# The same steps in another order: banded attention with block summaries, and a GELU MLP behind it

## The chip, the cores and the metric

The kernel runs on one core of a Trainium2 chip. The core has five engines that run side by side and meet only at semaphores: TensorE (PE) multiplies matrices, VectorE (DVE), ScalarE (ACT) and GpSimd (POOL) work on elements, and SyncE (SP) issues most of the transfers. The metric is the device time of one execution in microseconds (us). Runs of one kernel lie close together: the three of the kernel before lie between 559.98 and 560.04 us.

## What is computed

The reference, cut to what matters: an attention in which every query sees the keys less than 16 positions away and, beside them, one summary for each block of 32 keys (the maximum of the keys, the mean of the values), and an MLP with a GELU on its result.

```python
B, H, S, D = 4, 8, 768, 64;  block, window = 32, 16
k_sum = k.reshape(B, H, nb, block, D).max(axis=3)
v_sum = v.reshape(B, H, nb, block, D).mean(axis=3)
scores_l = where(abs(i - j) < window, q @ k.T / sqrt(D), -1e9)
scores_s = q @ k_sum.T / sqrt(D) + log(block)
a = softmax(concat(scores_l, scores_s));  out = a @ concat(v, v_sum)
x = out.transpose(0, 2, 1, 3).reshape(3072, 512)
h = x @ w_in                                  # w_in 512 x 2048
y = gelu(h) @ w_out                           # w_out 2048 x 512
```

## The kernel before

**Tiles.** The 3072 tokens are worked in batches (b, 0 to 3) and chunks of 256 tokens. The attention is cut into 24 units, each of four heads and four tiles of 64 queries; two units give one chunk of the MLP. PE multiplies 16-bit numbers: every 32-bit operand is split into a high and a low part (`_hi` on ACT or POOL, `_lo` on DVE), and a product of two operands is three matmuls. Chunks 0 to 3 of the MLP (argument c) go straight through `phase1`, `gelu` and `phase2`. The tokens behind them are multiplied by a scheme with sums and differences of blocks (Strassen's, `sp` for the first product and `so` for the second), which needs fewer matmuls and more work in sums: `xsum`, `snap`, `h_comb`, `h_gelu`, `h_sum`, `t_sum` and their `_hi` and `_lo` parts; `o_snap` (L1397), `o_sum` (L1404) and `o_out` (L1411) then collect the result from PSUM, and `o_put` (L1415) sends a piece of 128 by 256 numbers out.

**A unit's steps.** `scores` (PE, L861) multiplies queries and keys into the PSUM tile `pss`. `evac` (ACT, L877) or `add_mask` (DVE) fetch it, `maximum` (POOL, an all-reduce over partitions, L890), `shift` (DVE, L895) and `exponent` (ACT, L898) follow, then `s_p_hi`, `p_lo`, and on PE `values` and `sums`. `norm_take`, `norm_cross`, `norm_rec`, `norm_spread` and `norm_mult` divide by the sums, `x_hi` (ACT, L997) and `x_lo` (DVE, L1000) split the result for the MLP. A name with `f_` in front, `f_mask` and `m_shift` are the forms of the first three units; `s_k_hi` (ACT, L758) splits a unit's keys after `load_k` has brought them. `fill` steps are matmuls of ones, whose results nobody reads.

**The weights.** At the start DVE builds the split weights: `wi_bits` (three DVE steps, L477, L482, L486, for each of eight pieces that `fetch_w_in` brings), `wi_lo` (L515), `wo_bits`, `wo_lo` (L575), with `wi_hi` (L512) and `wo_hi` (L572) on ACT.

**What sets the order.** Nothing is scheduled by a planner on the way. `ORDER` (L79) is a string of 1,932 step names with arguments, and a loop at the end of the kernel calls them one after another. A step's instructions join the stream of their engine in this order, and each engine runs its stream in order; a DMA is issued by SP (or by ACT where the name has `a_` in front) in the order of its queue. Where two steps touch one tile the later in the list waits for the earlier. The table `SLOTS` says for each tag of small tiles (`f4k`, `g32`, `psh`, ...) which buffer the next tile of that tag takes, so that it depends on the order too. PSUM tiles are waited for as a whole: `o_snap b n j` reads the half j of the tile `pso_y`, `so b n q j` writes the half j, and a matmul that starts in one half waits for a reader of the other half that stands ahead of it.

In `so b n q j`, n is which of seven products (for one tile of results each), q the quarter of the inner dimension and j the half of 128 rows. With one and the same b and n, j the four quarters add up in the same PSUM tile. Six matmuls make one such step.

## Time and profile before

| | |
|---|---|
| time, median of three | 560.01 us (559.98 to 560.04) |
| the profiled execution | 560.75 us, of which the span is 558.9 us |
| granted TensorE clock, mean | 1.000 (2.4 GHz) |
| PE busy | 549.5 us (98%) |
| DVE busy | 484.0 us (87%) |
| ACT busy | 389.7 us (70%) |
| POOL busy | 110.8 us (20%) |
| bytes moved | 84.26 MB |

The profile cuts the span into stretches and says how long each engine was busy in each; it follows the chain of work that ended last back from the last instruction; and it lists the instructions of an engine in order of time, with the idle time ahead of each and what ended it. PE's busy time counts every matmul from its start to a modelled end, and matmuls overlap, so that PE can read as busy through a short gap; gaps are read from the starts.

### The profile page before, as it was taken

The page shows a single profiled execution, that of the slowest core. Times are in us where ns is not written, and L with a number is a line of the kernel's source. Part 1 is how long each engine was busy: PE and PEld are TensorE (multiplying, and loading weights), DVE is VectorE, ACT ScalarE, POOL GpSimd, SP SyncE. Part 2 cuts the span into 40 slices and gives each one's busy share as a digit, 9 for nine tenths or more (in the row PEclk, how much of TensorE's full clock was granted, in tenths as well). Part 3 has the DMA queues.
Part 4 walks back from the last instruction along what each step waited for, and adds up shares of the span by engine and source line. Part 5 has one row for each costly group of instructions (what it writes and reads, how often), then busy time and mean ns, then how long its engine had stood idle before and what let it go on. Part 6 is the DMA issues. An engine that isn't in the chain of part 4 may idle for free.

```text
span 558.9 us, 14486 instructions
## 1 busy us (share of the span) xinstructions
PE 549.5 (98%) x6155; PEld 414.8 (74%) x6155; DVE 484.0 (87%) x680; ACT 389.7 (70%) x677; POOL 110.8 (20%) x66
## 2 busy tenths in 40 slices
...
GB/s 328 396 285 380 166 173 178 280 116 221 157 146 171 153 143 187 133 65 182 127 167 149 154 115 89 90 145 200 256 207 150 60 94 1 1 1 29 48 1 86
DMA packets 42640, 84.26 MB, mean 151 GB/s; under 512 B 4176, under 2 KB 16720, under 8 KB 42064
## 3 DMA queue, kind: packets, MB, share of 16 engines
...
## 4 chain that ended last, share of the span: by engine, by line
PE 81%; DVE 13%; DMA 3%; issue 1%; ACT 1%; SPq 0%; DVEq 0%
PE psy L1091 15%; PE pso_y L1375 8%; PE psz L1091 8%; PE pso L1139 7%; PE pso L1140 7%; PE pso L1141 6%; PE psx L1091 4%; PE psd_y L1375 4%; PE pss_x L1375 4%; PE psv L943 3%; PE psh L1020 3%; PE psh L1021 2%; PE psh L1022 2%; PE pss L861 2%; PE psv_z L1375 2%; DMA w_out_h<-in_vt_dram 2%
## 5 line engine op out<-in xcount | busy, mean ns | idle before, releaser
L890 POOL PARTITION_ALL_REDUCE m<-s x23 | 82.0, 3567 | 187.4 <-DVE w_out_l L575 40.1
L1091 PEld LDWEIGHTS <-wt 128*128 128x128 f16 x768 | 74.3, 98 | 10.2 <-issue 0.2
L1139 PE MATMUL pso<-w_out_h,gg 128*128 128x512 f16 x192 | 72.9, 379 | 0.0
L1141 PE MATMUL pso<-w_out_h,gg 128*128 128x512 f16 x192 | 72.8, 379 | 0.0
L1140 PE MATMUL pso<-w_out_l,gg 128*128 128x512 f16 x192 | 72.8, 379 | 0.0
L1021 PE MATMUL psh<-xos,ww 128*128 128x256 f16 x256 | 69.8, 273 | 0.8 <-DVE xos L1000 0.8
L1091 PE MATMUL psy<-xos,wt 128*128 128x256 f16 x576 | 70.5, 273 | 0.0
L1020 PE MATMUL psh<-xos,ww 128*128 128x256 f16 x256 | 69.8, 273 | 0.1
L1022 PE MATMUL psh<-xos,ww 128*128 128x256 f16 x256 | 69.8, 273 | 0.0
L1091 PEld LDWEIGHTS <-ww 128*128 128x128 f16 x576 | 55.8, 98 | 8.9 <-issue 0.4
L1375 PEld LDWEIGHTS <-gg 128*128 128x128 f16 x576 | 55.8, 98 | 7.7 <-issue 1.1
L1102 ACT ACTIVATE ww<-psy 128x512 f32<-128x512 f32 x48 | 28.3, 591 | 27.4 <-PE psy L1091 27.3
L1141 PEld LDWEIGHTS <-gg 128*128 128x128 f16 x192 | 18.7, 98 | 22.8 <-issue 0.4
L1139 PEld LDWEIGHTS <-gg 128*128 128x128 f16 x192 | 18.7, 98 | 19.8 <-issue 0.4
L1140 PEld LDWEIGHTS <-gg 128*128 128x128 f16 x192 | 18.8, 98 | 19.1
L1375 PEld LDWEIGHTS <-wt 128*128 128x128 f16 x288 | 28.1, 98 | 3.4 <-issue 0.2
L1218 DVE SCALAR_TENSOR_TENSOR gg<-h,gg 128x512 f16<-128x512 f32 x32 | 21.4, 686 | 10.1 <-ACT gg L1215 9.9
L1020 PEld LDWEIGHTS <-ww 128*128 128x128 f16 x256 | 25.0, 98 | 4.3 <-issue 0.4
L1022 PEld LDWEIGHTS <-ww 128*128 128x128 f16 x256 | 25.0, 98 | 4.1 <-issue 1.2
L1021 PEld LDWEIGHTS <-ww 128*128 128x128 f16 x256 | 25.0, 98 | 3.7
L1029 ACT ACTIVATE g<-psh 128x512 f32<-128x512 f32 x32 | 19.0, 593 | 11.4 <-DVE gg L1038 8.6
L895 DVE TENSOR_TENSOR s<-s,m 128x1024 f32<-128x1024 f32 x21 | 25.5, 1216 | 0.1
...
## 6 DMA issues: line engine op xcount, KB each, us to landing
...
```

The source lines that it names most:

```text
L890: nc.gpsimd.partition_all_reduce(out_ap=self.m32, in_ap=self.s32, channels=P, reduce_op=bass_isa.ReduceOp.max)
L895: nc.vector.tensor_tensor(out=self.s32, in0=self.s32, in1=self.m32, op=ALU.subtract)
L1020: nc.tensor.matmul(ph[:, e, :], wh, xh, start=(k == 0), stop=False)
L1021: nc.tensor.matmul(ph[:, e, :], wh, xl, start=False, stop=False)
L1022: nc.tensor.matmul(ph[:, e, :], wl, xh, start=False, stop=(k == NCC - 1))
L1091: nc.tensor.matmul(ps[:, e, :], ws, xx, start=(first and e == 0 and k == 0 and m == 0), stop=(k == 1 and m == 2), skip_group_check=True,)
L1102: nc.scalar.activation(snaps[b, q, n], split8(acc[b, q, "y"]), AF.Copy)
L1139: nc.tensor.matmul(p, gh, w_out_h[:, f, :], start=(f == 0), stop=False)
L1140: nc.tensor.matmul(p, gh, w_out_l[:, f, :], start=False, stop=False)
L1141: nc.tensor.matmul(p, gl, w_out_h[:, f, :], start=False, stop=(f == NFC - 1))
L1218: nc.vector.scalar_tensor_tensor(out=a_part(b, q, m, 1), in0=h_src(b, q, m), scalar=SC_G, in1=a_part(b, q, m, 0), op0=ALU.mult, op1=ALU.su ...
L1375: nc.tensor.matmul(ps, g, ww_, start=(first and e == 0 and k == 0), stop=(e == 1 and k == 2), skip_group_check=True,)
```

## The change

The change moves steps in `ORDER` and writes `SLOTS` anew for that order. The list has the same 1,932 steps as before, and every engine has the same instructions; 1,726 steps stand at another place, most of them by a few places. No function is touched. Ten more lines of text in the table move the line numbers of all code behind it by 10: L1375 of before is L1385 of after. Two pieces of the diff:

```diff
-norm_take 1, x_lo 0, wi_bits 3 0, f_values 1, wi_bits 3 1, load_k 4, f_mask 3, norm_cross 1, scores 3, evac 3,
...
+norm_take 1, x_lo 0, wi_bits 3 0, wi_bits 3 1, f_mask 3, norm_cross 1, scores 3, s_k_hi 4, evac 3, norm_rec 1,
```

On ACT, near the start (some 34 us in): `evac 3` is the row with L877 (L887 after), `s_k_hi 4` the row with L758 (L768), `x_hi 1` the one with L997 (L1007), `wi_hi` the one with L512 (L522). Before:

```order
L877 ACTIVATE s32_3_456<-pss_3_399 128x1024
L512 ACTIVATE ww_93<-wt_94 128x8x128
L758 ACTIVATE k_all_100<-k32_4_397 128x10x64
L997 ACTIVATE xos_96<-x32s_95 128x512
L815 ACTIVATE qh_4_477<-q32_4_368 128x512
L512 ACTIVATE ww_93<-wt_94 128x8x128
```

And now:

```order
L768 ACTIVATE k_all_100<-k32_4_363 128x10x64
L887 ACTIVATE s32_3_442<-pss_3_384 128x1024
L522 ACTIVATE ww_93<-wt_94 128x8x128
L1007 ACTIVATE xos_96<-x32s_95 128x512
L825 ACTIVATE qh_4_477<-q32_4_353 128x512
L522 ACTIVATE ww_93<-wt_94 128x8x128
```

`s_k_hi 4`, which splits the keys that `load_k 4` brings, stood behind `evac 3` and `wi_hi 5` and now stands ahead of both; `x_hi 1` follows `wi_hi 5` directly.

On PE, where `so 3 4 0 0` and `so 3 4 0 1` begin (some 399 us in): L1091 (L1101) is a matmul of `sp 4 1 1` before and of `sp 4 0 1` now, and L1375 (L1385) the matmuls of the two `so` steps, six each; what a row waits for stands in brackets. Before:

```order
L1091 LDWEIGHTS ww_93
L1091 MATMUL psy_4_1_6274<-xos_96,ww_93 128x256
L1375 LDWEIGHTS gg_99 [waits DMAHW7_49]
L1375 MATMUL pso_y_3_5492<-wt_94,gg_99 128x256 [waits Activation_49]
...
L1375 LDWEIGHTS gg_99
L1375 MATMUL pso_y_3_5492<-wt_94,gg_99 128x256
L1375 LDWEIGHTS gg_99
L1375 MATMUL pso_y_3_5492<-wt_94,gg_99 128x256 [waits Activation_49]
```

And now:

```order
L1101 LDWEIGHTS ww_93
L1101 MATMUL psy_4_0_6282<-xos_96,ww_93 128x256
L1385 LDWEIGHTS gg_99 [waits DMAHW5_49]
L1385 MATMUL pso_y_3_5475<-wt_94,gg_99 128x256 [waits Activation_49]
...
L1385 LDWEIGHTS gg_99
L1385 MATMUL pso_y_3_5475<-wt_94,gg_99 128x256
L1385 LDWEIGHTS gg_99
L1385 MATMUL pso_y_3_5475<-wt_94,gg_99 128x256
```

Before, each of the two `so` steps waited for ACT, the second for `o_snap 3 3 1`, which stood between them in the list; now both `o_snap 3 3 0` and `o_snap 3 3 1` stand ahead of the first, and only the first waits. In the list `so 3 7 3 0`, `sp 4 1 1`, `o_snap 3 3 0`, `so 3 4 0 0`, `o_snap 3 3 1`, `so 3 4 0 1` has become `so 3 7 3 0`, `sp 4 0 1`, `o_snap 3 3 0`, `o_snap 3 3 1`, `so 3 4 0 0`, `so 3 4 0 1`.

On PE again, some 6 us from its end: `psd_y` is written by `so 5 7 3 1`, `pss_x` by `so 5 3 2 1` (its last row) ahead of it and by `so 5 3 0 1` behind it. Now:

```order
L1385 LDWEIGHTS wt_94
L1385 MATMUL pss_x_5_7934<-w_out_h_97,wt_94 128x256
L1385 LDWEIGHTS wt_94
L1385 MATMUL psd_y_5_7885<-t3_3_6597,wt_94 128x256
...
L1385 LDWEIGHTS wt_94
L1385 MATMUL psd_y_5_7885<-t3_3_6597,wt_94 128x256
L1385 LDWEIGHTS wt_94
L1385 MATMUL pss_x_5_7934<-w_out_h_97,wt_94 128x256 [waits DVE_49]
```

`o_sum 5 0` (DVE) reads the tile `pss_x`. It now stands between `so 5 3 2 1` and `so 5 7 3 1`, so that it waits for the former and `so 5 3 0 1` waits for it. Before, it stood ahead of `so 5 3 3 1`, `so 5 3 2 1` and `so 5 3 0 1` alike, with six matmul steps between it and the first of these, and that first one's row is the one that waited for it:

```order
L1375 MATMUL psv_z_5_8193<-w_out_l_98,gg_99 128x256
L1375 LDWEIGHTS gg_99
L1375 MATMUL psv_z_5_8193<-w_out_h_97,gg_99 128x256
L1375 LDWEIGHTS wt_94
L1375 MATMUL pss_x_5_7975<-w_out_h_97,wt_94 128x256 [waits DVE_49]
```

And on SP, the last issues of the program, all of them `o_put` (L1415, L1425 after). The tile `g32_os_5_1` is the result of `o_sum 5 0`, `g32_os_5_2` that of `o_sum 5 1`, `g32_os_5_3` that of `o_sum 5 3`, and `g32_os_5_5` those of `o_out 5 0` and `o_out 5 1`. Before:

```order
L1415 DMA out_0_dram<-g32_os_5_1_8065 128x256
L1415 DMA out_0_dram<-g32_os_5_3_8230 128x256
L1415 DMA out_0_dram<-g32_os_5_1_8065 128x256
L1415 DMA out_0_dram<-os_4_2_7417 128x256
L1415 DMA out_0_dram<-g32_os_5_3_8230 128x256
L1415 DMA out_0_dram<-g32_os_5_2_8158 128x256 x2
L1415 DMA out_0_dram<-g32_os_5_5_8342 128x256 x2
```

And now:

```order
L1425 DMA out_0_dram<-g32_os_5_1_8025 128x256
L1425 DMA out_0_dram<-g32_os_5_3_8192 128x256
L1425 DMA out_0_dram<-g32_os_5_5_8327 128x256
L1425 DMA out_0_dram<-g32_os_5_1_8025 128x256
L1425 DMA out_0_dram<-os_4_2_7506 128x256
L1425 DMA out_0_dram<-g32_os_5_3_8192 128x256
L1425 DMA out_0_dram<-g32_os_5_2_8139 128x256 x2
L1425 DMA out_0_dram<-g32_os_5_5_8327 128x256
```

The piece of `o_out 5 0` (the first row with `g32_os_5_5` now, `o_put 5 2 0`) has moved from next to last to the head of a row of seven issues; the piece of `o_out 5 1` is last in both.

## Rows read from the trace of the kernel before

**Rows 1.** The page, part 1: busy time, share of the span and instructions of each engine

```profile
PE 549.5 (98%) x6155; PEld 414.8 (74%) x6155; DVE 484.0 (87%) x680; ACT 389.7 (70%) x677; POOL 110.8 (20%) x66
```

**Rows 2.** Stretches (from:to, length), busy time of each engine, clock, DMA share, GB/s

```profile
20.00:40.00 20.00, 18.45 (x244) 10.78 (x241) 19.45 (x23) 16.13 (x34) 13.13 (x4) 1.00 0.90 330
...
120.00:140.00 20.00, 20.00 (x248) 11.48 (x247) 19.85 (x26) 14.57 (x23) 3.23 (x1) 1.00 0.63 187
...
380.00:420.00 40.00, 39.53 (x531) 33.66 (x530) 35.34 (x50) 28.24 (x54) 8.86 (x4) 1.00 0.76 225
...
540.00:559.00 19.00, 15.56 (x143) 13.70 (x140) 2.67 (x4) 1.43 (x4) 0.00 (x0) 1.00 0.19 63
```

**Rows 3.** The chain that ended last, 98 to 112 us (start, length, what)

```profile
107.81 0.70 DVE xos L1000
...
108.55 0.27 PE psh L1021
```

**Rows 4.** PE's waits: line, waited for, us in total, times, longest

```profile
PE pso_y L1375 <- ACT g_os L1397: 0.5, 1, 0.5
```

**Rows 5.** Order of time, PE, 398 to 402 us (start, length, line, operation, tiles)

```profile
398.93 0.82 PE L1375 MATMUL pso_y<-wt,gg 128*128 128x256 f16 x6
400.22 1.47 PE L1375 MATMUL pso_y<-wt,gg 128*128 128x256 f16 x12 [0.47 <-ACT g_os L1397]
```

**Rows 6.** Order of time, ACT, 398 to 402 us

```profile
399.78 0.38 ACT L1397 ACTIVATE g_os<-pso_y 128x256 f32<-128x256 f32 x1 [1.58 <-PE pso_y L1375]
```

**Rows 7.** Order of time, PE, 189.5 to 193 us

```profile
191.13 0.38 PE L1140 MATMUL pso<-w_out_l,gg 128*128 128x512 f16 x1
191.34 0.38 PE L1141 MATMUL pso<-w_out_h,gg 128*128 128x512 f16 x1
191.66 0.20 PE L861 MATMUL pss<-qh,k_all 64*128 64x64 f16 x2
```

**Rows 8.** Order of time, DVE, 377 to 389 us

```profile
381.93 0.69 DVE L1218 SCALAR_TENSOR_TENSOR gg<-g,gg 128x512 f16<-128x512 f32 x1 [1.06 <-ACT gg L1215]
...
384.87 0.69 DVE L1218 SCALAR_TENSOR_TENSOR wt<-g,wt 128x512 f16<-128x512 f32 x1
385.48 1.22 DVE L918 SCALAR_TENSOR_TENSOR vl<-v,vh 128x1024 f16<-128x1024 f32 x1
```

**Rows 9.** Order of time, PE, 386.5 to 388.5 us

```profile
387.68 0.38 PE L1375 MATMUL psh_w<-w_out_h,wt 128*128 128x256 f16 x2
```

**Rows 10.** Order of time, PE, 548 to 559 us

```profile
551.35 0.27 PE L1375 MATMUL pss_x<-w_out_h,wt 128*128 128x256 f16 x1
...
552.77 2.78 PE L1375 MATMUL psd_y<-t,gg 128*128 128x256 f16 x24
```

**Rows 11.** Order of time, DVE, 544 to 559 us

```profile
551.66 0.69 DVE L1404 SCALAR_TENSOR_TENSOR g_os<-pss_x,g_os 128x512 f32<-128x512 f32 x1 [0.61 <-PE pss_x L1375]
```

**Rows 12.** Order of time, SP's issues, 551 us to the end

```profile
551.35 0.45 SPq L1415 DMA_DIRECT2D out_dram<-os  x1
551.84 4.50 SPq L1415 DMA_DIRECT2D out_dram<-g_os  x5
...
556.00 0.33 SPq L1415 DMA_DIRECT2D out_dram<-g_os  x1
```

**Rows 13.** Order of time, ACT, 33 to 41 us

```profile
33.63 1.02 ACT L877 ACTIVATE s<-pss 128x1024 f32<-128x1024 f32 x1 [0.45 <-PE pss L861]
...
36.12 0.74 ACT L758 ACTIVATE k_all<-k 128x640 f16<-128x640 f32 x1 [0.38 <-DMA k<-in_kd_dram]
```

**Rows 14.** Order of time, DVE, 19.5 to 39 us

```profile
20.14 2.58 DVE L482 SCALAR_TENSOR_TENSOR wt<-x32s,wt 128x1024 int32<-128x1024 int32 x1
...
27.68 0.69 DVE L477 TENSOR_SCALAR wt<-gg 128x1024 int32<-128x1024 int32 x1 [0.28 <-DMA gg<-in_w_in_dram]
28.41 1.23 DVE L482 SCALAR_TENSOR_TENSOR wt<-gg,wt 128x1024 int32<-128x1024 int32 x1
...
38.54 0.68 DVE L1000 TENSOR_TENSOR xos<-x32s,xos 128x512 f16<-128x512 f32 x1
```

**Rows 15.** Order of time, POOL, 19.5 to 24 us

```profile
19.75 3.22 POOL L890 PARTITION_ALL_REDUCE m<-s  x1 [4.63 <-ACT s L877]
```

More of the change, by code (lines that the diff above doesn't have):

```diff
@@ L90 @@
-norm_rec 1, fetch_w_in 1 1, norm_spread 1, load_v 4, wi_hi 5, wi_bits 3 2, fill 10, s_k_hi 4, f_sums 2, norm_mult 1,
-x_hi 1, s_q_hi 4, norm_take 2, k_lo 4, wi_hi 3, x_lo 1, maximum 3, load_k 5, wi_lo 5, fill 2, wi_bits 1 0, f_mask 4,
-norm_cross 2, f_values 2, load_v 3, phase1 0 4, fetch_k 1 3, gelu 0 4, q_lo 4, phase1 0 0, wi_bits 1 1, phase1 0 5,
-shift 3, wi_hi 2, load_vs 3, wi_bits 1 2, norm_rec 2, load_vs 4, scores 4, exponent 3, norm_spread 2, wi_lo 3, wi_hi
-1, g_hi 0 4, fetch_w_in 6 2, norm_mult 2, prep_k 1 3, f_sums 3, wi_lo 2, gelu 0 0, norm_take 3, load_q 5, x_hi 2,
@@ L95 @@
-norm_cross 3, f_values 3, wi_lo 1, wi_bits 6 0, gelu 0 5, norm_rec 3, x_lo 2, fetch_k 1 0, fetch_w_in 7 3, norm_spread
-3, prep_k 1 0, evac 4, g_hi 0 5, maximum 4, norm_mult 3, phase1 0 3, s_k_hi 5, phase1 0 1, x_hi 3, fetch_w_out 0 4,
-g_hi 0 0, wi_bits 6 1, phase1 0 2, s_q_hi 5, k_lo 5, gelu 0 3, fetch_w_out 1 5, x_lo 3, phase1 1 4, q_lo 5, shift 4,
-exponent 4, wi_bits 6 2, load_k 6, g_lo 0 4, f_mask 5, gelu 0 1, wo_bits 0 0, s_k_hi 6, f_sums 4, g_lo 0 0, scores 5,
-wo_bits 0 1, wi_bits 7 0, load_v 5, g_hi 0 3, g_lo 0 5, f_values 4, gelu 0 2, g_hi 0 1, phase1 1 1, wo_bits 0 2,
@@ new lines @@
+norm_take 2, wi_hi 3, k_lo 4, x_lo 1, maximum 3, load_k 5, load_v 4, fill 2, wi_lo 5, wi_bits 1 0, f_mask 4,
+norm_cross 2, f_values 2, load_v 3, phase1 0 4, gelu 0 4, fetch_w_in 6 2, q_lo 4, phase1 0 0, phase1 0 5, wi_bits 1 1,
+shift 3, wi_hi 2, load_vs 3, wi_bits 1 2, norm_rec 2, norm_spread 2, load_vs 4, exponent 3, f_sums 3, wi_lo 3, scores
+4, wi_hi 1, g_hi 0 4, norm_mult 2, prep_k 1 3, wi_lo 2, load_q 5, x_hi 2, gelu 0 0, norm_take 3, wi_bits 6 0, f_values
+3, fetch_k 2 1, wi_lo 1, norm_cross 3, phase1 0 3, fetch_k 1 0, fetch_w_in 7 3, x_lo 2, norm_rec 3, g_hi 0 0, g_lo 0
```

395 lines of the change are left out of this document (205 added, 190 removed).

## The prediction

> **What bounds the kernel now.** I read the page's busy times first: PE is busy for 549.5 of 558.9 us, DVE for 484.0 [rows 1]. That says that PE bounds the kernel as a whole, not that it does so everywhere. The stretches tell it apart: from 20 to 40 us PE is busy for 18.45 of 20 us and DVE for 19.45, so the start is paced by DVE, which builds the split weights; from 120 us on PE is busy all the time (20.00 of 20), with one dent, 39.53 of 40 us from 380 to 420 [rows 2]. The chain of work that ended last shows where the one regime passes into the other: DVE's `x_lo 5` runs from 107.81 us, and the matmul of `phase1 2 6` that needs it starts at 108.55 us; from there the chain is PE's [rows 3]. So there are three places where an order can gain or lose: DVE's work ahead of `x_lo 5` and what stretches it, gaps on PE behind 108.55 us, and what follows PE's last matmul. The clock was at its full level (1.00) in every stretch read here [rows 2], so no term comes from it.
>
> On PE a gap shows in the distance of two starts. The matmuls of `so 3 4 0 0`, six of them, start from 398.93 us, and at the 0.11 us at which such matmuls follow each other the next would start at 399.59; it starts at 400.22 [rows 5]. That is a gap of 0.63 us, the only wait for another engine that the list of waits shows with L1375 [rows 4]: `o_snap 3 3 1` runs from 399.78 for 0.38 us, released by PE itself [rows 6].
>
> **The change, step by step.** No instruction comes or goes, so PE's own work is the same, and only waits, gaps and the two ends count.
>
> 1. The start: 0. Ahead of `x_lo 5` DVE has the very same instructions in both orders, and so has PE ahead of `phase1 2 6`; they stand in another order among themselves. DVE is all but never idle there, so the sum of durations sets when `x_lo 5` ends, and the order can change it only through DVE's idle time (one wait of 0.28 us for a transfer of weights) and through operations that last longer beside POOL: one `wi_bits` operation took 2.58 us beside an all-reduce that runs from 19.75 to 22.97 us, where its like takes 1.23 [rows 14, 15]. Which operations meet an all-reduce changes with the order in both directions. I take 0, and one such meeting more or fewer, plus or minus 1.35 us, as the bounds.
>
> The Trainium skill (SBUF — State Buffer, Who interferes with whom) says that GpSimd and some DVE operations share a pair of ports under an exclusive lock, and that the loser is blocked for the whole of the other's instruction. By that one meeting could cost up to the 3.22 us of the all-reduce; the row shows 1.35 us, so the measured stretch is what I use, and by the page alone the bounds would be 3.2 us to either side.
>
> 2. `so 3 4`: -0.63. Both `o_snap`s now stand ahead of `so 3 4 0 0`, and `sp 4 0 1` (12 matmuls, 12 x 0.11 = 1.31 us) stands between `so 3 7 3 0`, which releases them, and `so 3 4 0 0`. The last matmul's own 0.27 us, two copies of 0.38 [rows 6] and about 0.1 of handing over make 1.13 us behind that matmul's start, and PE arrives 0.11 + 1.31 = 1.42 us behind it. The wait goes, with 0.3 us to spare; ahead of the copies ACT has `exponent 21` and `s_p_hi 21`, which by the work ahead of them are through about a microsecond earlier.
>
> 3. `so 5 3 0 1`: +0.29. `o_sum 5 0` now waits for `so 5 3 2 1`, and `so 5 3 0 1` for `o_sum 5 0`. An `o_sum` takes 0.69 us and starts 0.31 behind the start of the matmul it waits for (551.35 to 551.66) [rows 10, 11]; with 0.05 to hand over PE may go on 1.05 us behind that matmul. In between it has only `so 5 7 3 1`, 6 x 0.11 = 0.65, and the 0.11 of the matmul itself: 0.76. The difference, 0.29 us, stands on PE with nothing behind it to hide it.
>
> 4. Switches: +0.5. Where PE goes from 128 x 128 matmuls to an attention block, it loses time without waiting for anyone: the matmuls start 0.21 us apart (191.13, 191.34), and the first of `scores` comes 0.32 us behind the last of them (191.66) [rows 7], 0.1 us more. I counted the places in the two orders behind `phase1 2 6`: 37 before, 42 after. Five more are 0.5 us; the trace shows such a gap at nearly all places of before.
>
> 5. `h_lo 3 3 4`: +0.3. Before, it runs from 384.87 to 385.56 us, and the matmul that needs it at 387.68 [rows 8, 9]. Now three operations more stand between `h_lo 3 3 12` (381.93) and it, `v_lo 20` with 1.22 us and two of the size of an `h_lo`, 0.69 each, 2.6 us in all [rows 8], and its matmul is 0.65 us earlier (one step fewer is ahead of it). If `h_lo 3 3 12` starts where it did, the part is ready at 388.1 at most and the matmul waits up to 1.0 us. But DVE idled 1.06 us ahead of `h_lo 3 3 12`, for ACT, [rows 8]; one sum of 0.68 us moves into that idle time, and so the chain behind it can run that much earlier. Between 0 and 1.0 I take 0.3, since the earlier chain takes 0.7 off the 1.0.
>
> 6. The end: +0.3. PE's last matmul ends at 552.77 + 2.78 = 555.55 us, and the last issue of SP is at 556.00, 0.45 behind it [rows 10, 12]. SP's issues follow each other at 0.49 us (551.35, 551.84) when released [rows 12]. Now `o_put 5 2 0`, which needs `o_out 5 0`, heads a row of seven issues. Four matmul steps stand behind the one that releases `o_out 5 0`, 4 x 0.65 = 2.62 us; with 0.42 for the copy and its release it is done 2.2 us ahead of PE's end. Six issues behind it at 0.49 put the last one at -2.15 + 2.94 = +0.8 behind PE's end, 0.3 later than before. At 0.45 us each it would be +0.1, at 0.55 +0.7.
>
> The sum is 0 - 0.63 + 0.29 + 0.5 + 0.3 + 0.3 = +0.76 us. The profiled execution took 560.75 us (span 558.9), and would take 561.5; it was 0.74 us above the median of the runs, 560.01. Against that median the forecast is 560.01 + 0.76, **560.8 us**, with 560.0 to 561.4 from the bounds of terms 5 and 6.
>
> **Rivals.**
>
> A. The start gets shorter. If two operations of DVE fewer meet an all-reduce, at 1.35 us each [rows 14], `x_lo 5` comes 2.7 us earlier and all of PE's work with it: 558.1 us. For it: DVE is the bound up to 108 us, and every tenth saved there reaches the end. Against: DVE is busy nearly throughout [rows 2], so an all-reduce that no longer meets one of its operations meets another; whether that one is stretched depends on its kind.
>
> B. The start gets longer, at one place. `s_k_hi 4` now stands ahead of `evac 3` on ACT. Before, `evac 3` ran at 33.63 us, and `s_k_hi 4` waited for `load_k 4` until 36.12 [rows 13]. If the keys land as late as that again, `evac 3` (1.02 us [rows 13]) and `wi_hi 5`, of the same size, stand behind 36.86, `x_hi 1` starts near 38.9, and `x_lo 1` comes near 39.5 instead of 38.54 [rows 14]: DVE idles for 1.0 us, and the time is 561.8. It decides from a landing at 35.1 us. For it: the row. Against: the load is issued at a place that lets it land earlier by my reckoning of what its queue has ahead of it, by 34.5.
>
> C. The order does what its table is made for and transfers land ahead of their readers. All of DVE's waits for a transfer behind 20 us come to 0.28 [rows 14], so that this gives 560.5 at best. The Trainium skill (Runtime: NRT & Kernel Launch, Instruction fetch mechanics) says that instructions are fetched in blocks ahead of their use and that crossing a block is mostly hidden; by that, too, there is little to gain, and no row that I use shows PE waiting for its own instructions.
>
> D. The new order changes nothing that counts: terms 3 to 6 are each hidden by something that I did not see, and the wait of term 2 alone goes: 559.4.
>
> **How the numbers follow.** The forecast has a chance of 0.48, A 0.17, B 0.18, C 0.07, D 0.10. A measurement of this kernel can tell about 0.2% from no change, 1.1 us: faster is below 558.9, slower above 561.1. A lies below; of D's cases a small part does too: faster 0.18. B lies above, and so does the upper part of the forecast's own range (561.1 to 561.4), with 0.12 of its 0.48: slower 0.30. The rest, 0.52, is no change. The range for 8 in 10 reaches towards A until about half of it is in, 558.7, and takes in B: 562.0.
>
> **What would show it.** Right: no gap on PE at `so 3 4 0 1`; a gap of 0.3 us at `so 5 3 0 1`, some 6 us ahead of PE's end; the last issue 0.7 to 0.8 us behind PE's end; `phase1 2 6` near 108.5 us. Wrong: `phase1 2 6` more than 1 us away from there, which would be A or B; for B `evac 3` on ACT behind a wait for keys, for A `wi_bits` or `wi_lo` operations near 1.2 us where they took 2. A gap at `so 3 3 3 1` of 1 us would say that I sized term 5 too low. Any gap of 0.6 us or more on PE behind 110 us that is not named here would make the prediction wrong.

## The result: 565.81 us, slower by 1.0%

The changed kernel takes 565.81 us (median of four runs, 564.37 to 566.14), and the kernel before, timed beside it, 560.02 us (median of four, 559.98 to 560.24). In 76 later runs, beside the experiments, the kernel before lay between 559.70 and 563.77 us: its runs do not lie as close together as the first three. The ratio is 1.0098 with a 95% interval of 1.0079 to 1.0116 (here and below a ratio is formed over all runs of the two kernels, so it is not quite the quotient of the medians). The forecast was 560.8 us with a range up to 562.0: too low by 5.0 us, and the time lies outside the range. The profiled execution took 565.54 us with a span of 563.8, which is 4.8 us more than that of before (560.75 and 558.9).

The page of the changed kernel, parts 1 and 4 (the chain that ended last, by engine), is to be read beside [rows 1]:

```profile
PE 552.2 (98%) x6155; PEld 414.6 (74%) x6155; DVE 485.9 (86%) x680; ACT 387.1 (69%) x677; POOL 104.5 (19%) x66
...
PE 45%; DVE 32%; DMA 9%; ACT 7%; issue 4%; SPq 1%; DVEq 0%; ACTq 0%
```

Part 4 of the kernel before:

```profile
PE 81%; DVE 13%; DMA 3%; issue 1%; ACT 1%; SPq 0%; DVEq 0%
```

DVE's share of the chain has grown from 13 to 32% of the span, some 180 us, so that DVE is on it behind 110 us too. Busy time tells little: PE has the same instructions and 2.7 us more of busy time in a span that is 4.8 us longer. The stretches say more (columns as in [rows 2]):

```profile
20.00:40.00 20.00, 17.58 (x237) 10.38 (x236) 18.59 (x22) 14.68 (x28) 10.82 (x4) 1.00 0.91 327
...
120.00:140.00 20.00, 19.77 (x197) 11.46 (x197) 19.20 (x23) 13.81 (x24) 3.22 (x1) 1.00 0.52 152
...
380.00:420.00 40.00, 38.77 (x519) 33.10 (x518) 36.06 (x50) 25.59 (x44) 10.56 (x4) 1.00 0.74 216
...
540.00:564.00 24.00, 20.12 (x183) 17.62 (x181) 4.66 (x7) 3.59 (x8) 0.00 (x0) 1.00 0.15 50
```

From 20 to 40 us DVE, which paces the start, is busy for 18.59 us where it was 19.45. From 120 to 140 us PE, which was busy all the time, has a dent (19.77 of 20), and the dent of 380 to 420 has become deeper, 38.77 instead of 39.53. The clock is at its full level (1.00) in all of them.

PE's waits for other engines in the changed kernel (line, waited for, total, times, longest; the longer wait of the first row lies ahead of 108 us; of before, [rows 4] had one of 0.5 us behind 110 us):

```profile
PE psh L1031 <- DVE xos L1010: 1.0, 2, 0.7
...
PE pso_y L1385 <- DMA wt<-t_dram: 0.9, 1, 0.9
...
PE psy L1101 <- DVE xos L1073: 0.4, 1, 0.4
...
PE psh_w L1385 <- DVE wt L1228: 0.3, 1, 0.3
PE psn L969 <- DVE pl L920: 0.3, 1, 0.3
...
PE psv L953 <- DVE vl L928: 0.2, 1, 0.2
```

These are idle times. The time that PE loses is read from the distance of two starts and is longer, since the modelled end of the matmul ahead covers a part. I went through all starts of PE behind 108 us in both traces. The sum, by starts, for the one profiled execution of each kernel:

| place | us | in the prediction |
|---|---|---|
| the start: `x_lo 5` at 108.74 instead of 107.81 | +0.94 | term 1: 0 |
| five waits between 110 and 310 us (`phase1 2 1` 0.27, `values 6` 0.40, `sums 14` 0.44, `sp 2 3 7` 0.16, `sp 3 0 7` 0.55) | +1.82 | none |
| `so 3 3 3 1` waits for `h_lo 3 3 4` and what follows it | +0.51 | term 5: +0.3 |
| `so 3 7 2 0` waits for a transfer | +1.05 | none |
| `sp 5 2 5` | +0.23 | none |
| `so 5 3 0 1` waits for `o_sum 5 0` | +0.29 | term 3: +0.29 |
| `so 3 4 0 1` no longer waits | -0.63 | term 2: -0.63 |
| switches, 42 instead of 37, 0.094 to 0.096 each | +0.47 | term 4: +0.5 |
| sum | +4.68 | |

PE's last matmul ends at 560.24 instead of 555.55, 4.69 us later, so the table accounts for it. The issues of SP behind it add 0.27 (below), and from the last issue to the end of the span it takes 0.14 less: 4.8 us of span.

The wait that is gone: `so 3 4 0 0` and `so 3 4 0 1` are now twelve matmuls in a row, where [rows 5] had six and a gap:

```profile
403.71 1.47 PE L1385 MATMUL pso_y<-wt,gg 128*128 128x256 f16 x12
```

**The start.** SP's issues, 9 to 23 us (start, length, line, what). First the kernel before, then the changed one:

```profile
10.20 0.34 SPq L685 DMA_DIRECT2D q<-in_qd_dram  x1
10.58 0.91 SPq L631 DMA_DIRECT2D w_out_h<-in_vt_dram  x2
11.53 0.43 SPq L694 DMA_DIRECT2D v<-in_vw_dram  x1
18.61 0.33 SPq L685 DMA_DIRECT2D q<-in_qd_dram  x1
```

```profile
10.68 0.43 SPq L641 DMA_DIRECT2D w_out_h<-in_vt_dram  x1
18.70 0.33 SPq L695 DMA_DIRECT2D q<-in_qd_dram  x1
19.07 1.37 SPq L641 DMA_DIRECT2D w_out_h<-in_vt_dram  x1
20.48 0.43 SPq L704 DMA_DIRECT2D v<-in_vw_dram  x1
```

The `q` row is `load_q 3`. It waits for its buffer until 18.6 or 18.7 us in both orders. Before, `fetch_vt 2` and `load_v 0` were ahead of it and left at about 11 us. Now they stand behind it, and leave at 19.07 and 20.48. What the transfers did meanwhile, in stretches of 2 us, first the changed kernel, then the one before (last two columns: busy share of the DMA engines, GB/s):

```profile
20.00:22.00 2.00, 1.91 (x31) 1.76 (x30) 2.00 (x2) 0.97 (x2) 2.00 (x1) 1.00 0.81 183
```

```profile
20.00:22.00 2.00, 1.78 (x31) 1.65 (x28) 2.00 (x2) 0.97 (x2) 2.00 (x1) 1.00 1.03 409
```

183 GB/s instead of 409 are 0.45 MB less in these 2 us, nearly half a piece of the weights. The piece that `wi_bits 2 0` reads landed at 28.61 us instead of 27.66, and DVE waited 1.13 us where it had waited 0.28 [rows 14]:

```profile
28.63 0.69 DVE L487 TENSOR_SCALAR wt<-gg 128x1024 int32<-128x1024 int32 x1 [1.13 <-DMA gg<-in_w_in_dram]
```

**The middle.** The wait of `values 6` has three rows. The changed kernel in order of time, POOL's all-reduce, then DVE, then PE:

```profile
136.12 3.22 POOL L900 PARTITION_ALL_REDUCE m<-s  x1 [28.49 <-DVE ks L620]
```

```profile
136.65 1.65 DVE L556 TENSOR_TENSOR t<-wt,t 128x256 f32<-128x256 f32 x1
138.21 1.21 DVE L928 SCALAR_TENSOR_TENSOR vl<-v,vh 128x1024 f16<-128x1024 f32 x1
```

```profile
139.48 0.22 PE L953 MATMUL psv<-ph,vl 128*64 128x64 f16 x2 [0.23 <-DVE vl L928]
```

`v_lo 6` ends at 139.42 and PE, which had come to `values 6`, waits for it. Ahead of it `wt_add 1 1` took 1.65 us beside the all-reduce, and 0.43 in the trace of before. Operations that are stretched beside an all-reduce stand ahead of two more of the waits: `sg_lo 2 0 2` (1.90 us instead of 0.69) 14 us ahead of that of `sums 14`, and `t_sum 1 1` (1.15 instead of 0.69) 3 us ahead of that of `sp 3 0 7`. That they cause these waits is not shown.

**The transfer.** PE at 398.80 us, and SP's issues ahead of it, 388 to 392 us (changed kernel):

```profile
398.80 0.81 PE L1385 MATMUL pso_y<-wt 128*128 128x256 f16 x6 [0.89 <-DMA wt<-t_dram]
```

```profile
388.32 0.32 SPq L1344 DMA_DIRECT2D t_dram<-tst  x1
388.69 0.43 SPq L704 DMA_DIRECT2D v<-in_vw_dram  x1
389.21 0.39 SPq L1277 DMA_DIRECT2D wt<-t_dram  x1
389.65 0.43 SPq L1293 DMA_DIRECT2D wt<-wt_dram  x1
390.12 1.23 SPq L1277 DMA_DIRECT2D wt<-t_dram  x2
```

`so 3 7 2 0` needs the piece of weights that `tl 3 2 3` brings, the second of the last two issues. Five issues stand ahead of it within 2.3 us, `load_v 23` among them; it left at 390.64 and landed at 398.76, 8.1 us later. In the trace of before `load_v 23` left at 386.76 and `tl 3 2 3` at 389.38; it landed at 393.25, after 3.9 us, and was first read at 393.69: 0.44 us to spare, which no row of before had shown as a wait. The transfer was not sent later, seen from PE: it left 7.1 us before PE came to `so 3 7 2 0` (397.75), and 4.3 us before its first reader in before. It was sent into a fuller queue: from 392 to 398 us the 16 DMA engines were busy throughout (a share of 1.02 to 1.09 in each 2 us), while before they had a share of 0.66 to 0.70 from 388 to 392.

**The end.** PE's last rows, and SP's last issue:

```profile
552.59 0.82 PE L1385 MATMUL psd_y<-t,wt 128*128 128x256 f16 x6
553.53 0.27 PE L1385 MATMUL pss_x<-w_out_h,wt 128*128 128x256 f16 x1
...
557.46 2.78 PE L1385 MATMUL psd_y<-t,gg 128*128 128x256 f16 x24
```

```profile
560.96 0.40 SPq L1425 DMA_DIRECT2D out_dram<-g_os  x1
```

The six matmuls of `so 5 7 3 1` begin at 552.59, and `so 5 3 0 1` at 553.53, 0.94 us later instead of 0.65: the gap of 0.29 that term 3 gave. The row of seven issues begins at 558.07, 2.17 ahead of PE's end, and its last one at 560.96, 0.72 behind it, 0.48 us from one to the next; term 6 said 2.15, 0.8 and 0.49. Before, the last issue was 0.45 behind.

### The profile page after: what moved, and what is told of

Same layout as the page of the kernel before. It is cut to its first block, busy times and chain, and to the rows that moved or that the text cites. A ratio compares the mean times of both kernels' runs of the same rounds, so it can differ in the third digit from the quotient of the medians.

```text
span 563.8 us, 14486 instructions
## 1 busy us (share of the span) xinstructions
PE 552.2 (98%) x6155; PEld 414.6 (74%) x6155; DVE 485.9 (86%) x680; ACT 387.1 (69%) x677; POOL 104.5 (19%) x66
## 4 chain that ended last, share of the span: by engine, by line
PE 45%; DVE 32%; DMA 9%; ACT 7%; issue 4%; SPq 1%; DVEq 0%; ACTq 0%
PE psy L1101 7%; PE pso_y L1385 5%; PE psz L1101 4%; PE pss_x L1385 3%; PE psd_y L1385 3%; PE pso L1149 3%; PE pso L1150 3%; PE pso L1151 3%; PE psx L1101 2%; DVE gg L1228 2%; PE psv L953 2%; DMA xos<-in_w_out_dram 2%; DVE gg L1048 2%; DVE wst L492 2%; DMA w_out_h<-in_vt_dram 2%
## 5 line engine op out<-in xcount | busy, mean ns | idle before, releaser
L900 POOL PARTITION_ALL_REDUCE m<-s x23 | 78.5, 3415 | 213.1 <-DVE pl L920 59.1
L1101 PEld LDWEIGHTS <-wt 128*128 128x128 f16 x768 | 74.1, 98 | 11.2 <-issue 1.2
L1101 PE MATMUL psy<-xos,wt 128*128 128x256 f16 x576 | 70.5, 273 | 0.4 <-DVE xos L1073 0.4
L1101 PEld LDWEIGHTS <-ww 128*128 128x128 f16 x576 | 55.6, 98 | 8.6 <-issue 0.8
L1385 PEld LDWEIGHTS <-gg 128*128 128x128 f16 x576 | 56.3, 98 | 6.7 <-issue 0.2
L1385 PEld LDWEIGHTS <-wt 128*128 128x128 f16 x288 | 27.7, 98 | 5.5 <-issue 1.6
L1039 ACT ACTIVATE g<-psh 128x512 f32<-128x512 f32 x32 | 18.6, 591 | 12.3 <-DVE gg L1048 9.2
```

What stands on the lines that cost most here:

```text
L900: nc.gpsimd.partition_all_reduce(out_ap=self.m32, in_ap=self.s32, channels=P, reduce_op=bass_isa.ReduceOp.max)
L1101: nc.tensor.matmul(ps[:, e, :], ws, xx, start=(first and e == 0 and k == 0 and m == 0), stop=(k == 1 and m == 2), skip_group_check=True,)
L1385: nc.tensor.matmul(ps, g, ww_, start=(first and e == 0 and k == 0), stop=(e == 1 and k == 2), skip_group_check=True,)
```

## Experiments

All kernels below have the line numbers of before.

**Thirds of the order.** The two lists hold the same set of steps in their first 319 places, and again in their first 1,025, so that a kernel can change from one order to the other there. Each of three kernels takes one third from the new order and the rest from the order before (in SLOTS the names of buffers are joined accordingly).

```diff
 start_only:   steps 0 to 318 new,  the rest as before
 middle_only:  steps 319 to 1024 new,  the rest as before
 end_only:     steps 1025 to 1931 new,  the rest as before
```

> The first 319 steps in the new order (both orders have the same steps there), all others as before. Theory S (the queue of SP): load_q 3, which waits for a buffer until 18.7 us, now stands ahead of fetch_vt 2 and load_v 0, the transfers run dry, the piece of weights for wi_bits 2 lands at 28.6 instead of 27.7 us, and the whole kernel is 0.9 us later: 560.9 to 561.0 us, with DVE idle for 1.1 us ahead of wi_bits 2 0. Rival P (operations beside an all-reduce last longer): only what k_lo 4 lost, 0.4 us, comes through: 560.4 us.

> Steps 320 to 1025 in the new order, the others as before (110 to about 310 us). Theory M: the waits of PE that the trace of the changed kernel shows there (0.27, 0.40, 0.44, 0.16 and 0.55 us) belong to this part of the order, whatever the start does, and five more switches cost 0.47 us: about 2.3 us slower, 562.3 us. Rival: the waits come from the later start alone, which shifts DVE against the transfers; then only the switches remain, 560.5 us.

> Steps from 1026 on in the new order, the others as before. Theory E: the waits at so 3 3 3 1 (0.51), so 3 7 2 0 (1.05), sp 5 2 5 (0.23) and so 5 3 0 1 (0.29), less the one at so 3 4 0 1 (0.63), plus 0.2 behind PE's end: 1.65 us slower, 561.7 us. Rival: the wait at so 3 7 2 0 for a transfer is one of the shifted clock of the earlier parts and goes: 560.6 us.

| | median (range, runs) | ratio [95%] |
|---|---|---|
| start_only | 562.26 us (561.01 to 563.17, 10) | 1.0029 [1.0015, 1.0042] |
| middle_only | 562.83 us (562.28 to 564.78, 9) | 1.0042 [1.0026, 1.0057] |
| end_only | 561.30 us (560.89 to 562.41, 10) | 1.0013 [1.0000, 1.0026] |

The kernel before had a median of 560.10 us beside them. Each third costs something, the last one at the edge of what can be told (its interval begins at 1.0000), and the three add up to 0.84% of the 0.98%. The middle, of which the prediction has no term, costs most. It showed waits of 0.28, 0.61, 0.37, 0.44 and 0.16 us at `phase1 2 1`, `values 6`, `sums 13`, `sums 14` and `sp 2 3 7`, 1.86 us in all, where the whole new order had 1.82 with a slightly different list. They are not the work of a late start: `start_only`, with `x_lo 5` at 108.84, has none of them. `end_only` has the waits of `so 3 3 3 1` (0.46), `so 3 7 2 0` (0.78), `sp 5 2 5` (0.22) and `so 5 3 0 1` (0.29), and not that of `so 3 4 0 1`. In `start_only`, whose end is that of before, `so 3 7 2 1` waited 1.39 us for its transfer: the margin of 0.44 us can be used up without any change of the queue next to it. With the 1.03 us by which `x_lo 5` is late it makes up the 2.4 us by which PE ends later in that profile. It also bears on the miss of this run's theory (561.0): the ten runs lie in two groups, 561.01 to 561.91 and 562.61 to 563.17, 1.5 us apart in the mean, and the profiled one, with the wait, is in the upper. That the wait makes the upper group is likely and not shown.

**`load_q 3`.** Two kernels move this one step, in the new order back behind `load_v 0`, and in the order before ahead of `fetch_vt 2`.

```diff
 after_loadq, against the new order
-fetch_vt 1, f_sums 0, load_q 3, f_scores 2, fetch_vt 2, evac 1, prep_k_end 0 1, k_lo 3, load_v 0,
+fetch_vt 1, f_sums 0, f_scores 2, fetch_vt 2, evac 1, prep_k_end 0 1, k_lo 3, load_v 0, load_q 3,
 before_loadq, against the order before
-fetch_vt 1, f_sums 0, fetch_vt 2, evac 1, prep_k_end 0 1, load_v 0, f_scores 2, k_lo 3, load_q 3,
+fetch_vt 1, f_sums 0, load_q 3, fetch_vt 2, evac 1, prep_k_end 0 1, load_v 0, f_scores 2, k_lo 3,
```

> The changed kernel with one step moved back: load_q 3 behind fetch_vt 2 and load_v 0, as it stood before. Theory S: SP no longer holds the two transfers back until 18.7 us, DVE's wait ahead of wi_bits 2 0 falls from 1.13 us to 0.3, phase1 2 6 waits until 108.6 us instead of 109.5, and the time is 0.9 us below the changed kernel's. Rival: the start was late for another reason (the operations beside an all-reduce), and phase1 2 6 stays at 109.4.

> The kernel before with load_q 3 alone moved, ahead of fetch_vt 2 and load_v 0. Theory S: the transfers run dry from 20 to 22 us (some 180 instead of 400 GB/s), wi_bits 2 0 waits 1.1 instead of 0.3 us, and the kernel is 0.9 us slower: 561.0 us. Rival: the order of SP's queue doesn't count, since the same bytes come before the weights: 560.0 us.

`after_loadq`: 563.29 us (562.89 to 563.69, 4 runs), ratio 1.0048 [1.0033, 1.0063], beside 1.0098 for the whole change. That is 2.5 us between the medians where the theory said 0.9. The two profiles differ by 1.84 us at PE's end: `x_lo 5` is 0.99 earlier, `sp 3 0 7` no longer waits (0.55), and `so 3 7 2 0` and `so 3 3 3 1` wait 0.81 and 0.31 instead of 1.05 and 0.51, so that waits further on went with the late start. The transfers are back, and the wait at `wi_bits 2 0` is gone:

```profile
20.00:22.00 2.00, 2.00 (x29) 1.61 (x28) 2.00 (x2) 0.97 (x2) 2.00 (x1) 1.00 1.03 409
```

`before_loadq`: 560.75 us (560.01 to 562.15, 10 runs), ratio 1.0006 [0.9994, 1.0018]. The same hole opens:

```profile
20.00:22.00 2.00, 1.90 (x33) 1.77 (x30) 2.00 (x2) 0.97 (x2) 2.00 (x1) 1.00 0.71 167
```

and DVE waits 1.02 us at `wi_bits 2 0`. But the time hardly follows. In its profile `wi_bits 1 2`, a later operation, is not stretched as it was before, which gives 0.84 us back, and `x_lo 5` starts at 107.86, where it started at 107.81. The stretch goes with who begins first, DVE or a copy on POOL (L716). In order of time, first the kernel before, then `before_osnap` (below), which has the same start:

```profile
43.61 1.12 POOL L716 COPY v<-w_out_h 24x1024 f32<-24x1024 f32 x1 [4.34 <-DMA v<-in_vw_dram]
...
43.76 2.05 DVE L486 SCALAR_TENSOR_TENSOR wt<-gg,wt 128x1024 int32<-128x1024 int32 x1
```

```profile
43.73 1.21 DVE L486 SCALAR_TENSOR_TENSOR wt<-gg,wt 128x1024 int32<-128x1024 int32 x1
...
43.88 1.96 POOL L716 COPY v<-w_out_h 24x1024 f32<-24x1024 f32 x1 [4.63 <-DMA v<-in_vw_dram]
```

In `before` and `end_only` the copy begins first, `wi_bits 1 2` takes 2.05 us and `x_lo 5` starts at 107.81 and 107.94; in `before_osnap`, `osnap_again` and `before_two` DVE begins first, `wi_bits 1 2` takes 1.21, and `x_lo 5` starts at 106.92 to 106.99. Against these three `before_loadq` has lost 0.9 us at `x_lo 5`, the 0.9 of its theory. So the cause of the late weights is shown in both directions. Its price on the end, half a per cent in the new order and less than the times can tell in the order before, depends on what else an execution of the start loses.

**The start with rival B taken out as well.**

```diff
 after_start: after_loadq, and
-scores 3, s_k_hi 4, evac 3, norm_rec 1, fetch_w_in 1 1, norm_spread 1, wi_hi 5,
+scores 3, evac 3, norm_rec 1, fetch_w_in 1 1, norm_spread 1, wi_hi 5, s_k_hi 4,
```

> The changed kernel with load_q 3 moved back and s_k_hi 4 put behind evac 3 and wi_hi 5 again. Theory B: evac 3 and wi_hi 5 no longer stand behind the keys of load_k 4, so that DVE's wait ahead of x_lo 1 (0.7 to 1.5 us where load_q 3 or tl 3 2 3 alone was moved) goes; x_lo 5 begins at 107.0 to 107.8 us. Rival: x_lo 1 waits for x_hi 1 behind another operation, and the wait stays.

563.69 us (563.48 to 564.05, 4 runs), ratio 1.0062 [1.0049, 1.0076]. That is not below `after_loadq`, whose interval overlaps, though the mechanism did what B says: no idle time ahead of `x_lo 1` (0.73 us in `after_loadq`), and `x_lo 5` at 107.32 instead of 107.75. In the changed kernel the keys did land late, with the rows that answer to [rows 13]:

```profile
35.55 0.74 ACT L768 ACTIVATE k_all<-k 128x640 f16<-128x640 f32 x1 [1.66 <-DMA k<-in_kd_dram]
36.19 1.01 ACT L887 ACTIVATE s<-pss 128x1024 f32<-128x1024 f32 x1
```

and the idle time of DVE that follows shows in four of the experiments with `s_k_hi 4` at its new place, here `after_tl` (`x_lo 1` was at 38.54 before [rows 14]):

```profile
39.46 1.11 DVE L1000 TENSOR_TENSOR xos<-x32s,xos 128x512 f16<-128x512 f32 x1 [1.23 <-ACT xos L997]
```

So B happens, but its price, 0.4 us between these two profiles, is less than the start differs between executions of one order (below), and the times don't show it; `after_seven`, in which both steps are moved back as well, has `x_lo 5` at 107.77.

**The transfer of `tl 3 2 3`.** It goes ahead of `tl 3 1 4`, three places earlier in its queue.

```diff
 after_tl, against the new order
-h_lo 3 3 3, so 3 5 1 1, tl 3 1 4, ..., norm_cross 20, tl 3 0 4, tl 3 2 3, load_vs 23,
+h_lo 3 3 3, so 3 5 1 1, tl 3 2 3, tl 3 1 4, ..., norm_cross 20, tl 3 0 4, load_vs 23,
```

> The changed kernel with tl 3 2 3 moved ahead of tl 3 1 4, so that it is issued ahead of three other transfers. Theory: it lands some 3 us earlier, the wait of 1.05 us at so 3 7 2 0 goes, and the time falls by 1.0 us. Rival: a later step on PE (so 3 4 0 0, or scores 23, whose keys come behind) waits instead, and nothing is won.

564.58 us (563.91 to 564.62, 4 runs), ratio 1.0068 [1.0051, 1.0085]; the whole change has 1.0098. The wait of `so 3 7 2 0` is gone, and `so 3 7 3 1` waits 0.68 us in its place for the piece that is now behind. A part of the 1.05 us comes back, a part moves on. The medians differ by 1.2 us, more than the 0.4 that is left of it; in this profile `x_lo 5` is 0.52 us earlier than in that of the changed kernel, which this edit doesn't touch.

**`values 6`.** My theory P was that the all-reduce's stretch of `wt_add 1 1` makes `v_lo 6` late. `prep_k 2 0`, DVE work that was behind, goes ahead of it.

```diff
 after_prepk, against the new order
-phase2 0 7, norm_take 6, prep_v 2 1, g_hi 2 1, ..., g_lo 2 4, norm_cross 6, prep_k 2 0, gelu 2 3,
+phase2 0 7, norm_take 6, prep_k 2 0, prep_v 2 1, g_hi 2 1, ..., g_lo 2 4, norm_cross 6, gelu 2 3,
```

> The changed kernel with prep_k 2 0 moved ahead of prep_v 2 1 on DVE, where it stood before, so that maximum 7 (POOL), which waits for it, starts some 3 us earlier. Theory P: the all-reduce then runs beside reductions with one input, as before, wt_add 1 1 takes 0.43 instead of 1.65 us, and the wait of 0.40 us at values 6 goes: 0.4 us faster. Rival: DVE is late there by its own work, wt_add 1 1 gains nothing that another operation doesn't lose, and the wait stays.

565.09 us (564.69 to 566.27, 4 runs), ratio 1.0084 [1.0067, 1.0101], not to be told from the whole change. The wait of `values 6` is gone. Yet the stretch is not: the all-reduce now meets `g_lo 2 1`.

```profile
134.28 3.58 POOL L890 PARTITION_ALL_REDUCE m<-s  x1 [24.71 <-ACT rc L974]
```

```profile
135.19 1.89 DVE L1038 SCALAR_TENSOR_TENSOR gg<-g,gg 128x512 f16<-128x512 f32 x1
...
139.07 0.41 DVE L546 TENSOR_TENSOR t<-wt,t 128x256 f32<-128x256 f32 x1
```

`wt_add 1 1` takes its 0.41 us again and `g_lo 2 1` 1.89 instead of 0.69. About 1.2 us are lost to the all-reduce either way. What `prep_k 2 0` gave is an idle time of DVE of 0.69 us ahead of `prep_v 2 1`, which it fills. As a cause of this wait the stretch falls, since an all-reduce still costs DVE its 1.2 us there and the wait is gone; the idle time that the new order leaves on DVE stands.

**All of it undone, and then the middle too.** `after_seven` joins the edits so far with three more at the places of terms 5, 3 and 6. `after_mid` moves back two of the middle's operations in the new order; `after_ten` has both, with `tl 3 2 3` ahead of `ts 3 4`.

```diff
 after_seven: after_start, after_tl, after_prepk, and
-x_lo 17, load_v 23, h_hi 3 3 4, so 3 5 0 1, h_lo 3 3 3, so 3 5 1 1, tl 3 1 4, h_lo 3 3 4, so 3 3 3 1,
+load_v 23, h_hi 3 3 4, so 3 5 0 1, so 3 5 1 1, tl 3 2 3, tl 3 1 4, h_lo 3 3 4, x_lo 17, h_lo 3 3 3, so 3 3 3 1,
-so 5 3 3 1, so 5 3 2 1, o_sum 5 0, so 5 7 3 1, so 5 3 0 1,
+o_sum 5 0, so 5 3 3 1, so 5 3 2 1, so 5 7 3 1, so 5 3 0 1,
-o_sum 5 1, o_put 5 2 0, o_out 5 1, o_put 5 0 0, ..., o_put 5 1 1, o_put 5 2 1
+o_sum 5 1, o_out 5 1, o_put 5 0 0, ..., o_put 5 1 1, o_put 5 2 0, o_put 5 2 1
 after_mid, against the new order
-prep_v 1 2, k_lo 7, wo_bits 6 0, phase1 2 4, g_lo 1 7, gelu 2 6,
+prep_v 1 2, wo_bits 6 0, phase1 2 4, g_lo 1 7, k_lo 7, gelu 2 6,
-sg_hi 2 1 2, t_sum 0 1, t_sum 0 0, load_k 18, p_lo 14, sg_lo 2 1 2,
+sg_hi 2 1 2, load_k 18, p_lo 14, t_sum 0 1, t_sum 0 0, sg_lo 2 1 2,
```

> The changed kernel with the steps behind seven of its losses moved back: load_q 3, s_k_hi 4, tl 3 2 3, prep_k 2 0, h_lo 3 3 3 and x_lo 17 behind h_lo 3 3 4, o_sum 5 0, o_put 5 2 0. Theory: what is left above the kernel before are PE's waits at phase1 2 1 (0.27), sums 14 (0.44), sp 2 3 7 (0.16), sp 3 0 7 (0 to 0.55), sp 5 2 5 (0.22) and the switches (0.47), less the wait at so 3 4 0 1 (0.63): 560.9 to 561.5 us. Rival: the losses replace each other, and it stays above 563 us.

> The changed kernel with two small moves on DVE in the middle: k_lo 7 behind g_lo 1 7 (as before), and t_sum 0 1 and t_sum 0 0 behind p_lo 14. Theory D: two of PE's waits are DVE's order and nothing else. The load of ACT's table ahead of gelu 2 4 waits for g_lo 1 7, which k_lo 7 (0.8 us) holds back, and sums 14 waits for p_lo 14, which the sums (0.6 us each) hold back; both waits, 0.27 us at phase1 2 1 and 0.44 us at sums 14, go, and the time falls by 0.7 us. Rival: sums 14 is late because sg_lo 2 0 2 takes 1.90 us beside an all-reduce, and with that still there the wait only moves to the next step that DVE feeds.

> The changed kernel with the moves of the run with seven losses undone and these two, and tl 3 2 3 still earlier, ahead of ts 3 4. Theory: left over the kernel before are sp 2 3 7 (0.16), sp 3 0 7 (0.3), sp 5 2 5 (0.22) and the switches (0.47), less 0.63 at so 3 4 0 1: 560.5 us, and up to 561.5 where so 3 7 3 1 waits for its transfer as it did for 1.7 us in the run with seven. Rival: other losses come in place of these, and it stays above 562.

| | median (range, runs) | ratio [95%] |
|---|---|---|
| after_seven | 562.32 us (561.94 to 563.46, 5) | 1.0036 [1.0023, 1.0050] |
| after_mid | 565.88 us (564.01 to 567.77, 5) | 1.0090 [1.0062, 1.0117] |
| after_ten | 562.56 us (562.11 to 562.93, 7) | 1.0036 [1.0025, 1.0047] |

Seven edits take the loss from 0.98% to 0.36%. The theory of `after_seven` (560.9 to 561.5) is missed by 0.8 us or more; in its profile `so 3 7 3 1` waits 1.72 us for its transfer. The two of the middle take nothing more off that the times can tell, neither alone nor on top of the seven, and `after_ten` came as its rival said, above 562. PE's waits from 110 to 320 us in `after_mid`, beside the last rows of the list above (L1101, L969, L953 there are L1091, L959, L943 here):

```profile
PE psy L1091 <- ACT ww L1102: 0.7, 2, 0.5
PE psv L943 <- DVE vl L918: 0.7, 1, 0.7
PE psy L1091 <- DVE xos L1063: 0.4, 1, 0.4
PE psn L959 <- DVE pl L910: 0.2, 1, 0.2
```

The waits of `phase1 2 1` and `sums 14`, at which the edits aim, are gone. By starts there are now 0.82 us at `values 6`, 0.35 at `sums 13`, 0.28 at `sp 2 2 7`, 0.27 at `sums 15`, 0.64 at `sp 2 3 7` and 0.57 at `sp 3 0 7`: 2.93 us in place of 1.82. The two moves have changed which steps wait, and not for less time. In `after_ten` the waits that are left, 0.56 us at `sums 13`, 0.28, 0.27 and 0.64 at `sp 2 2 7`, `sums 15` and `sp 2 3 7`, 0.42 at `so 3 7 3 1` and 0.22 at `sp 5 2 5`, add up to 2.4 us. With -0.63 for `so 3 4 0 1` and +0.47 for the switches that makes +2.2; the medians differ by 2.25.

**The gain alone.** `before_osnap` takes only term 2 from the change, and `before_two` sends `tl 3 2 3` earlier too.

```diff
 before_osnap (and osnap_again), against the order before
-o_snap 3 3 0, so 3 4 0 0, x_lo 17, tl 3 2 4, o_sum 3 0, xs_lo 4 1, norm_rec 20, o_snap 3 3 1,
+o_snap 3 3 0, o_snap 3 3 1, so 3 4 0 0, x_lo 17, tl 3 2 4, o_sum 3 0, xs_lo 4 1, norm_rec 20,
 before_two: before_osnap, and
-v_lo 20, ts 3 4, maximum 21, ..., tl 3 3 3, tl 3 2 3, h_lo 3 3 3,
+v_lo 20, tl 3 2 3, ts 3 4, maximum 21, ..., tl 3 3 3, h_lo 3 3 3,
```

> The kernel before with one step moved: o_snap 3 3 1 directly behind o_snap 3 3 0, ahead of so 3 4 0 0. Theory: the wait of 0.63 us at so 3 4 0 1 goes and nothing takes its place: 559.4 us. Rival: scores 23 or the next step waits instead: 560.0 us.

> The kernel before with o_snap 3 3 1 directly behind o_snap 3 3 0, as once before, timed in more rounds. Theory: the wait of 0.63 us is gone for good, and the time is 0.6 us below the kernel before. Rival: the transfer for so 3 7 2 1, which had 0.44 us to spare, swallows part of it in most executions: 0.3 us or less.

> The same, and tl 3 2 3 moved ahead of ts 3 4 in SP's queue, so that it is issued some 7 us earlier. Theory: so 3 7 2 1 never waits for its transfer, which it did for 1.4 us in two of the kernels with a start like before: 559.4 us, with fewer executions above 561. Rival: the executions above 561 us come from the start, and their share stays.

| | median (range, runs) | ratio [95%] |
|---|---|---|
| before_osnap | 560.40 us (559.28 to 562.85, 10) | 1.0002 [0.9986, 1.0018] |
| osnap_again (the same kernel) | 559.94 us (559.22 to 561.00, 11) | 0.9987 [0.9974, 1.0001] |
| before_two | 559.37 us (559.18 to 561.3, 11) | 0.9986 [0.9977, 0.9995] |

The wait of `so 3 4 0 1` is gone in all three profiles, but `before_osnap` alone is not shown to be faster: the first comparison says no change, the second leaves it just open. With the transfer at an earlier place ten of eleven runs lie between 559.18 and 559.63, beside 560.41 for the kernel before; of `osnap_again`, timed with it, five of eleven lie below 559.63. The ratios of the two are alike (0.9986 and 0.9987), so that the earlier place seems to make the times steadier and is not shown to be a gain by itself. In the profile of `before_two`, with a span of 557.8 us, PE has one wait left behind 110 us, 0.25 us at `so 3 6 3 1`. This version beats both kernels, the one before by 0.14%.

## Why the prediction was wrong

**Term 1, the start (0; measured +0.94).** This is the step that failed first. It argued that DVE has the same instructions ahead of `x_lo 5`, and that the order can act only through DVE's idle time, "one wait of 0.28 us for a transfer of weights". The first half is true; the wait in the second became 1.13 us. The step compared what stands ahead on DVE, PE and ACT, and not the queue of SP, on which the weights travel. That `load_q 3` stood still for its buffer until 18.6 us was in the trace of before (the issue at 18.61, 7 us behind the one ahead of it), and that it was moved past two others was in the order. The bounds of plus or minus 1.35 held the size by chance: they were made for another mechanism, the stretch beside an all-reduce.

**The missing term, the middle (measured +1.82).** "Any gap of 0.6 us or more on PE behind 110 us that is not named here" was to make the prediction wrong. The middle has none of that size, but five smaller ones, and the sum put waits there at nothing without a reason. I read "PE is busy all the time" from 120 us on as slack of the engines that feed it. [rows 2] shows the opposite in the same line: DVE is busy for 19.85 of 20 us there. Two engines are full, and PE's full row says only that the order before had fitted DVE's work to PE's needs. A new order that leaves an idle 0.69 us on DVE, as ahead of `prep_v 2 1`, or puts an operation ahead of the one that PE needs, as at `sums 14`, has little to pay with. `middle_only` shows that the new middle costs 0.42% by itself, and `after_mid` that moving two of its operations back moved the waits. What makes each of the five waits is shown for `values 6`, `phase1 2 1` and `sums 14` alone, whose waits went with the moved step.

**A second missing term, the transfer (+1.05).** The prediction looked at transfers only where before showed a wait, in rival C. `tl 3 2 3` had 0.44 us to spare in before, and the new order put it behind more issues in a row. This gap is what the prediction named as a sign of being wrong, over 0.6 us on PE and not named. `after_tl` shows that its place in the queue sets the wait; `start_only` and `before_loadq` (1.36 us at `so 3 7 2 1`) show that this margin is gone in some executions of the old queue as well.

**Terms 2, 3, 4 and 6 (-0.63, +0.29, +0.5, +0.3; measured -0.63, +0.29, +0.47, +0.27).** These were right to 0.03 us each, and three of the four signs of being right came true with them (the fourth, `phase1 2 6` near 108.5 us, did not: 109.49). Each came from rows of before: a wait taken from starts, a matmul chain counted against an operation, a count of switches, and SP's issue rate. **Term 5 (+0.3; measured +0.51)** was on the right place and too small, within its bounds of 0 to 1.0: the idle time of DVE ahead of `h_lo 3 3 12` went from 1.06 to 0.68 us, so that it took in 0.4 of the chain where I had given it 0.7.

**The rivals.** A did not happen. B did: the keys came at 35.53, behind its threshold of 35.1; the earlier landing at 34.5 that I held against it was wrong. In the profile of the changed kernel the loss of 1.0 us ahead of `x_lo 1` does not show as such, since a stretched operation (`k_lo 4`, 1.73 us) ran there; undoing B in `after_start` made `x_lo 5` 0.43 us earlier and no measurable gain. C's mechanism came with the other sign, as a wait for transfers that grew. D had the gain of term 2 and nothing else; `before_osnap` is that case, and gave between -0.26 and +0.18%.

**The sum.** Terms 2 to 6 give +0.91 with their measured sizes (-0.63 + 0.29 + 0.47 + 0.51 + 0.27); the two missing ones, term 1 and the small `sp 5 2 5` make 4.04, and the last transfer gives 0.14 back. The prediction's range of 560.0 to 561.4 is not what the bounds of its terms 5 and 6 give: with 0 to 1.0 and 0.1 to 0.7 the sum runs from 560.3 to 561.9, and term 1's 1.35 us to either side are in neither. Even with them it stays below what was measured. The medians differ by 5.8 us and the two profiled executions by 4.8, since that of before was 0.74 us above its own median and that of the changed kernel 0.27 below. The former's start was late for its kind, by the stretch of `wi_bits 1 2` told above: in five of the six profiles with the start of before `x_lo 5` begins between 106.92 and 107.94 us, and in four of the five with the new one between 108.22 and 108.84 (one execution of each kind came some 2 us later). In these two the granted clock fell to its lower level (1.2 GHz, 0.50 of full speed) for some 3 us of the start; in the other nine it was at the full level throughout. `middle_only` had 0.50 from 11 to 13 us (0.76 and 0.53 in the microseconds to either side), after PE had been busy for 0.34, 0.72 and 1.00 of the three microseconds from 7 to 10. `after_prepk` had 0.50 from 40 to 43 us, after a busy time of 0.35, 0.00 and 0.36. From 107.4, the middle value of all six, to 108.83, that of all five, the new start costs 1.4 us rather than 0.94; set against the three executions without the stretch it is 1.8.

**Open.** Why an all-reduce stretches one of DVE's operations to some three times its length and leaves the next one alone was not settled. What makes `sums 13`, `sp 2 3 7` and `sp 3 0 7` late was read from the traces alone and not tried by itself. Why the effect of `load_q 3` on the times is half a per cent in one order and near nothing in the other rests on a few profiles of each. The change also gives small tiles other buffers (`SLOTS`); all kernels with a part of the new order have that part's buffers too, so that what the buffers cost apart from the order was not tried.
